# Gathering the transposes of a linear-attention pair behind the next projection, in a fused attention and FFN kernel

## The chip, the cores and the metric

One core of one Trainium2 chip. The metric is the device time of one execution in microseconds; the kernel before ran three times.

## The reference

Attention with a feature map of exponentials, over batch 8, 8 heads, 576 positions and 64 dimensions a head, followed by an FFN on the 4608 tokens (512 to 2048 to 512, with a learned leak `alpha`). All in float32.

```python
def phi(x):
    proj = np.einsum('bhsd,df->bhsf', x, w_phi)
    proj = proj - np.max(np.abs(proj), axis=-1, keepdims=True)
    return np.concatenate([np.exp(proj), np.exp(-proj)], axis=-1)
q_p, k_p = (phi(q), phi(k))
kv = np.einsum('bhsf,bhsd->bhfd', k_p, v)
z = np.sum(k_p, axis=2)
num = np.einsum('bhsf,bhfd->bhsd', q_p, kv)
den = np.einsum('bhsf,bhf->bhs', q_p, z)[..., None] + 1e-06
attn = num / den
...
h = x @ w_in
g = np.maximum(h, 0.0) + alpha * np.minimum(h, 0.0)
out = g @ w_out
```

## The kernel before, in words

**Attention** goes pair by pair: 32 pairs of two heads (`i` from 0 to 31). A pair's k and q come in one tile of nine times 128 columns, and `project(0)` and `project(1)` multiply them with `w_phi`. `project(0)` makes the first eight k tiles (two heads of four, into `pj`), `project(1)` the rest of k and all of q. VectorE takes the row maxima of the absolute values and subtracts them; ScalarE takes the exponentials of k (`k_exp`). `k_z` and `k_acc` then sum z and accumulate kv in one PSUM bank, `kv_out` copies that bank to `ks` on ScalarE, `kv_turn` transposes its three 128x128 blocks on TensorE (L380), and `kv_copy` copies the result to `sf`. `q_turn(0..2)` transposes the ten q blocks (L391, L394), four, four and two, and `q_exp` takes their exponentials straight out of PSUM into `qf`. A visit later `den` and `num` multiply `sf` with `qf`; `den` goes by way of DRAM to be inverted and spread, and GpSimd multiplies it in.

**The FFN** has its 16 hidden blocks in two parts. Five of them are computed during the attention phase, 512 tokens at a time, as `up` and `down` steps of three matmuls each with 512 columns (each value split in a high and a low part; L503 to L505 and L509 to L511). After an `up` ScalarE makes `r` and `g` (two relus, `parts`), VectorE joins them, ScalarE casts to `gh`, VectorE subtracts to `gl`. The other eleven hidden blocks follow when the attention is done, from about 520 us on. Weights are decoded from 64-bit words in between, on ScalarE, VectorE and GpSimd (`decode_*`).

**Order.** Every step is a closure with a time of its own, counted in visits: pair i's steps stand at `i +` the entries of `places(i)` (L57 to L84), the FFN's and the decoder's steps at times of their own. All are sorted by that key (L741, a stable sort of a list in which the pairs stand in order), and TensorE, ScalarE, VectorE and SyncE are pinned to that order. A visit at time t thus does for TensorE: `project(1)` of pair t, `k_z` of t−1, `den` of t−2, `k_acc` of t−1, `num` of t−2, `project(0)` of t+1, and then FFN steps among which the transposes of pair t−1 are strewn:

```python
p=(-0.9955 if early else -0.993, 0.0),
...
kr=1.10,
kc=1.16,
q=(1.34, 1.50, 1.20),
qe=(1.46, 1.62, 1.28),
```

`kr` is `kv_turn`, `kc` `kv_copy`, `q` and `qe` are `q_turn` and `q_exp` for 0, 1 and 2. `early` is i < 9 (`ZP`); the FFN begins at 9.23, so the visits before hold attention alone.

**PSUM** has eight banks of 512 float32 columns: two for the FFN (`psf`), two for `pj`, one for kv (`ps_kv`), and three in a ring (`ps_m`, tag `m`) for the last tiles of `project(1)`, `den`, `num`, and for the late pairs all transposes.

Of the kernel before, what the change touches and what calls it, by code (L numbers as in the profile page):

```python
# [8 lines left out]
F32 = mybir.dt.float32  # L9
# [7 lines left out]
P = 128  # L17
B, H, S, D = 8, 8, 576, 64
FD = 128
# [35 lines left out]
ZP = 9  # L55


def places(i):
    early = i < ZP
    end = i >= NPAIR - 2  # L60
    return dict(
        ld=-1.90,
        lv=-0.80,
        p=(-0.9955 if early else -0.993, 0.0),
        ke=(-0.26, 0.0011),
        ks=(0.0015, 0.0022, 0.0026),
        kz=1.0002,
        ka=1.0012,
        ko=1.0025,
        kr=1.10,  # L70
        kc=1.16,
        q=(1.34, 1.50, 1.20),
        qe=(1.46, 1.62, 1.28),
        d=2.0004,
        ds=2.0008,
        n=2.005,
        s=2.0055,
        d9=2.25,
        dv=3.0016 if early else 3.20 if end else 2.80,
        rd=3.0017 if early else 3.21 if end else 2.82,  # L80
        rr=3.20 if early else 3.45 if end else 3.001,
        x=3.45 if early else 3.60 if end else 3.20,
        xs=3.90 if early else 3.85 if end else 3.45,
    )  # L84
# [24 lines left out]
def fused_kernel(ctx: ExitStack, tc: tile.TileContext, kq, v, w_phi, w_in, w_out, alpha, out):  # L109
    nc = tc.nc  # L110
    act, dve, pool, pe = nc.scalar, nc.vector, nc.gpsimd, nc.tensor
# [18 lines left out]
    psf = ctx.enter_context(tc.tile_pool(name="psf", bufs=2, space=PSUM))  # L130

    ident = cst.tile([P, P], F32, name="ident")
# [122 lines left out]
    ps_m = ps_m_.enter_context(tc.tile_pool(name="ps_m", bufs=3, space=PSUM))  # L255
# [4 lines left out]
    st = att.enter_context(tc.tile_pool(name="st", bufs=2))  # L260
    ps_pj = att.enter_context(tc.tile_pool(name="ps_pj", bufs=1, space=PSUM))
    ps_kv = att.enter_context(tc.tile_pool(name="ps_kv", bufs=1, space=PSUM))
# [9 lines left out]
    def attention_units(i):  # L272
        b, hp = divmod(i, NP)
        c = {}
# [79 lines left out]
                    )  # L354

        def k_z():
            c["kv"] = ps_kv.tile([P, 3, FD], F32, tag="kv", name=f"kv{i}")
            if i < ZP:
                zs = [c["x", 0][:, :, :, j, :] for j in range(4)] + [c["x", 1][:, :, :, 0, :]]
            else:  # L360
                zs = [c["z"]]
            for j, z in enumerate(zs):
                for g in range(4):
                    h, a = divmod(g, 2)
                    pe.matmul(  # L365
                        c["kv"][32 * g : 32 * g + 32, 2],
                        lhsT=ones,
                        rhs=z[:, a, h, :],
                        start=j == 0,
                        stop=j == len(zs) - 1,  # L370
                    )

        def kv_out():
            c["ks"] = st.tile([P, 3, FD], F32, tag="ks", name=f"ks{i}", bufs=1)
            act.copy(c["ks"], c["kv"])

        def kv_turn():
            ps = c["kt"] = ps_m.tile([P, 3, P], F32, tag="m", name=f"kt{i}")
            for j in range(3):
                pe.transpose(ps[:, j, :], c["ks"][:, j, :], ident)  # L380

        def kv_copy():
            c["st"] = st.tile([P, 3, P], F32, tag="sf", name=f"sf{i}")
            act.copy(c["st"], c["kt"])

        def q_turn(h):
            pp, tag = (psf, "f") if i < ZP - 1 and h < 2 else (ps_m, "m")
            ps = c["qt", h] = pp.tile([P, 2 if h == 2 else 4, P], F32, tag=tag, name=f"qt{i}_{h}")
            if h == 2:
                for g in range(2):  # L390
                    pe.transpose(ps[:, g, :], c["t", 1][:, g, 0, :], ident)  # L391
            else:
                for j in range(4):
                    pe.transpose(ps[:, j, :], c["t", 1][:, h, 1 + j, :], ident)  # L394

# [69 lines left out]
        def store():  # L465
            nc.sync.dma_start(x_d[hp, :, b * S : (b + 1) * S], c["s"])

        at = places(i)
        us = [
            (at["ld"], load),  # L470
            (at["lv"], load_v),
            (at["ka"], k_acc),
            (at["kz"], k_z),
            (at["ko"], kv_out),
            (at["kr"], kv_turn),
            (at["kc"], kv_copy),
            (at["n"], num),
            (at["d"], den),
# [11 lines left out]
        for n in range(3):  # L490
            us.append((at["ks"][n], lambda n=n: k_sum(n)))
            us.append((at["q"][n], lambda n=n: q_turn(n)))
            us.append((at["qe"][n], lambda n=n: q_exp(n)))
# [308 lines left out]
```

## Time and profile before

| what | us |
|---|---|
| median of 3 runs | 1137.34 |
| lowest and highest | 1134.79, 1138.68 |
| the profiled execution | 1136.66 |
| its span, first to last instruction | 1134.9 |

The profile is of one execution. The spans of matmuls overlap, since they are pipelined and their ends are modelled; how TensorE's time is spent is read from start to start. PE is TensorE's matmuls, PEld its weight loads, DVE VectorE, ACT ScalarE, POOL GpSimd, SP SyncE, which only issues transfers. In the rows `h`, `o` are the FFN's tiles, `kt` and `qt` the transposed kv and q, `n` is `num`, `pj` the k tiles. L127 and L123 are helpers that every subtraction of a high part and every cast has in common.

### The profile page before, as it was taken

How to read it: one execution, taken by the hardware profiler on the slowest of the kernel's cores; microseconds unless marked ns; L12 is line 12 of the kernel's file. 1: busy time of each engine (PE TensorE's matmuls, PEld its weight loads, DVE VectorE, ACT ScalarE, POOL GpSimd, SP SyncE). 2: the span in 40 equal slices, each digit the busy share in tenths (PEclk: the TensorE clock that was granted, in tenths of full speed). 3: DMA queues.
4: the chain of work that ended last, by engine and by line, in shares of the span. 5: the costliest groups of instructions: out<-in, count | busy, mean ns of one | idle time of the engine just before them, and what ended most of it. 6: DMA issues, size and time to landing. Idle time of an engine off the chain costs nothing.

```text
span 1134.9 us, 18362 instructions
## 1 busy us (share of the span) xinstructions
PE 1114.9 (98%) x7232; PEld 866.8 (76%) x7232; DVE 639.5 (56%) x978; ACT 561.2 (49%) x1149; POOL 214.5 (19%) x219
## 2 busy tenths in 40 slices
PE   7999999999999999999999999999999999999998
PEld 5766777777777777677778888888888888888886
DVE  7888867798788877835762432424242433333323
ACT  4777656666666765664553332424333333333332
POOL 1345332322424142243552000000000000000000
PEclk8999999999999999999999999999999999999999
DMA  5466264556446365466626130303030302020021
GB/s 188 142 184 216 80 194 147 171 163 205 145 163 199 94 214 168 146 197 213 231 74 211 69 112 1 111 1 111 1 112 1 111 1 80 33 79 33 3 72 38
DMA packets 74101, 133.68 MB, mean 118 GB/s; under 512 B 14624, under 2 KB 24480, under 8 KB 73376
## 3 DMA queue, kind: packets, MB, share of 16 engines
q1 hardware_dynamic: 71712, 122.48, 33.4%
q0 software_dynamic: 2016, 9.96, 2.6%
q8 instruction: 57, 0.93, 0.3%
q14 instruction: 28, 0.23, 0.1%
q10 hardware_dynamic: 288, 0.07, 0.0%
HBM read 93.92 MB, written 38.42 MB: 117 GB/s over the span
## 4 chain that ended last, share of the span: by engine, by line
PE 92%; DVE 4%; DMA 2%; ACT 1%; issue 0%; SPq 0%; ACTq 0%; DVEq 0%
PE h L503 11%; PE h L505 11%; PE h L504 11%; PE po L511 8%; PE po L509 8%; PE po L510 8%; PE kv L348 6%; PE pj L307 5%; PE n L413 5%; PE o L511 3%; PE o L509 3%; PE o L510 3%; PE d L431 3%; PE qt L394 2%; PE kv L365 2%; PE pl L307 1%
## 5 line engine op out<-in xcount | busy, mean ns | idle before, releaser
L240 DVE SCALAR_TENSOR_TENSOR g<-r,aln,g 128x512 f32<-128x512 f32 x144 | 111.0, 771 | 320.1 <-ACT g L236 319.8
L235 ACT ACTIVATE r<-h 128x512 f32<-128x512 f32 x144 | 86.5, 601 | 286.0 <-PE h L505 285.8
L127 DVE TENSOR_TENSOR gl<-g,gh 128x512 fp32r<-128x512 f32 x144 | 105.5, 732 | 73.0 <-ACT gh L123 72.5
L123 ACT CAST gh<-g 128x512 fp32r<-128x512 f32 x144 | 90.1, 625 | 88.1 <-DVE g L240 88.1
L236 ACT ACTIVATE g<-h 128x512 f32<-128x512 f32 x144 | 85.8, 596 | 2.8 <-DMA part_d<-os 2.8
L509 PE MATMUL po<-gh,wd 128*128 128x512 f32 x216 | 84.3, 390 | 0.0
L511 PE MATMUL po<-gl,wd 128*128 128x512 f32 x216 | 84.3, 390 | 0.0
L510 PE MATMUL po<-gh,wd 128*128 128x512 f32 x216 | 84.3, 390 | 0.0
L311 DVE TENSOR_REDUCE m<-pj 128x8 f32<-128x1024 f32 (+1 forms) x66 | 78.2, 1185 | 7.0 <-PE pj L307 6.7
L307 PE MATMUL pj<-w_sb,raw 64*128 64x128 f32 x1024 | 74.2, 286 | 7.8 <-DMA w_sb<-w_phi_dram 4.1
L307 PEld LDWEIGHTS pj<-w_sb,raw 64*128 64x128 f32 x1024 | 65.0, 194 | 21.4 <-issue 14.1
L189 POOL TENSOR_TENSOR aw<-ew,aw 128x256 f32<-128x256 f32 x64 | 56.7, 887 | 128.6 <-DVE ew L184 128.6
L312 DVE TENSOR_TENSOR t<-pj,m 128x1024 f32<-128x1024 f32 (+1 forms) x66 | 78.7, 1192 | 2.3
L509 PE MATMUL o<-gh,w 128*128 128x512 f32 x180 | 75.9, 422 | 1.9 <-ACT os L554 1.7
L503 PE MATMUL h<-xh,w 128*128 128x512 f32 x180 | 75.8, 421 | 0.0
L463 POOL TENSOR_TENSOR s<-s,rr 128x576 f32<-128x576 f32 x32 | 48.5, 1517 | 140.6 <-DMA rr<-rec_d 120.2
L511 PE MATMUL o<-gl,w 128*128 128x512 f32 x180 | 71.6, 398 | 3.2 <-DVE gl L127 3.0
L511 PE MATMUL po<-gl,w 128*128 128x512 f32 x180 | 70.3, 391 | 1.5 <-DVE gl L127 1.4
L404 ACT ACTIVATE qf<-qt 128x512 f32<-128x512 f32 x128 | 68.5, 616 | 6.3 <-PE qt L394 6.3
L505 PE MATMUL h<-xl,w 128*128 128x512 f32 x180 | 70.7, 393 | 0.0
L510 PE MATMUL o<-gh,w 128*128 128x512 f32 x180 | 70.6, 392 | 0.0
L504 PE MATMUL h<-xh,w 128*128 128x512 f32 x180 | 70.5, 392 | 0.0
(105 smaller groups left out, 2408.8 us busy)
## 6 DMA issues: line engine op xcount, KB each, us to landing
xr<-x_d SPq DMA_DIRECT2D x18, 1024.0 KB
raw<-kq_dram SPq DMA_DIRECT2D x31, 576.0 KB
v<-v_dram SPq DMA_DIRECT2D x32, 320.0 KB
w_d<-raww SPq DMA_DIRECT2D x38, 256.0 KB
rr<-rec_d SPq DMA_DIRECT2D x64, 144.0 KB
x_d<-s SPq DMA_DIRECT2D x32, 288.0 KB
part_d<-os SPq DMA_DIRECT2D x36, 256.0 KB
pt<-part_d SPq DMA_DIRECT2D x9, 1024.0 KB
```

The costliest lines, as they stand in the source:

```text
L123: return act.copy(dst, src)
L127: return eng.tensor_tensor(dst, src, f(hi), op=ALU.subtract)
L235: act.activation(st["r"], ps, AF.Relu, scale=-1.0)
L236: act.activation(st["g"], ps, AF.Relu)
L240: dve.scalar_tensor_tensor(g, st["r"], aln[:, ff : ff + 1], g, op0=ALU.mult, op1=ALU.add)
L307: pe.matmul(dst[h, j], lhsT=c["raw"][hs, ts], rhs=w_sb[hs], start=True, stop=True)
L503: pe.matmul(ps, lhsT=wt[0][:, ws], rhs=xh, start=n == 0, stop=False)
L504: pe.matmul(ps, lhsT=wt[1][:, ws], rhs=xh, start=False, stop=False)
L505: pe.matmul(ps, lhsT=wt[0][:, ws], rhs=xl, start=False, stop=n == NK - 1)
L509: pe.matmul(ps, lhsT=wt[2][:, ws], rhs=gh, start=first, stop=False)
L510: pe.matmul(ps, lhsT=wt[3][:, ws], rhs=gh, start=False, stop=False)
L511: pe.matmul(ps, lhsT=wt[2][:, ws], rhs=gl, start=False, stop=last)
```

## The change

For pairs from 9 on, `kv_turn`, `q_turn` and `kv_copy` get keys between 1.0070 and 1.0074, and the exponentials of q the keys 1.10, 1.20 and 1.32. The two transposed blocks of kv and the two of q's third group share one four-slot tile `kq` in the ring; the transposed z goes to a fourth slot that the tile in kv's bank gets, and `kv_copy` becomes two copies. For pairs before 9 keys and steps stay as they were, with `kt` and the third `qt` now being parts of four-slot tiles.

```diff
-        kr=1.10,
-        kc=1.16,
-        q=(1.34, 1.50, 1.20),
-        qe=(1.46, 1.62, 1.28),
+        kr=1.10 if early else 1.0070,
+        kc=1.16 if early else 1.0074,
+        q=(1.34, 1.50, 1.20) if early else (1.0072, 1.0073, 1.0071),
+        qe=(1.46, 1.62, 1.28) if early else (1.20, 1.32, 1.10),
...
         def k_z():
-            c["kv"] = ps_kv.tile([P, 3, FD], F32, tag="kv", name=f"kv{i}")
+            c["kv"] = ps_kv.tile([P, 4, FD], F32, tag="kv", name=f"kv{i}")
...
         def kv_out():
             c["ks"] = st.tile([P, 3, FD], F32, tag="ks", name=f"ks{i}", bufs=1)
-            act.copy(c["ks"], c["kv"])
+            act.copy(c["ks"], c["kv"][:, 0:3])
 
         def kv_turn():
-            ps = c["kt"] = ps_m.tile([P, 3, P], F32, tag="m", name=f"kt{i}")
+            c["kq"] = ps_m.tile([P, 4, P], F32, tag="m", name=f"kq{i}")
             for j in range(3):
-                pe.transpose(ps[:, j, :], c["ks"][:, j, :], ident)
+                pe.transpose(c["kv"][:, 3] if j == 2 and i >= ZP else c["kq"][:, j], c["ks"][:, j, :], ident)
 
         def kv_copy():
             c["st"] = st.tile([P, 3, P], F32, tag="sf", name=f"sf{i}")
-            act.copy(c["st"], c["kt"])
+            if i < ZP:
+                act.copy(c["st"], c["kq"][:, 0:3])
+                return
+            act.copy(c["st"][:, 0:2], c["kq"][:, 0:2])
+            act.copy(c["st"][:, 2], c["kv"][:, 3])
 
         def q_turn(h):
-            pp, tag = (psf, "f") if i < ZP - 1 and h < 2 else (ps_m, "m")
-            ps = c["qt", h] = pp.tile([P, 2 if h == 2 else 4, P], F32, tag=tag, name=f"qt{i}_{h}")
             if h == 2:
+                if i < ZP:
+                    c["kq"] = ps_m.tile([P, 4, P], F32, tag="m", name=f"qt{i}_{h}")
+                ps = c["qt", h] = c["kq"][:, 2:4]
                 for g in range(2):
                     pe.transpose(ps[:, g, :], c["t", 1][:, g, 0, :], ident)
             else:
+                pp, tag = (psf, "f") if i < ZP - 1 else (ps_m, "m")
+                ps = c["qt", h] = pp.tile([P, 4, P], F32, tag=tag, name=f"qt{i}_{h}")
```

## Rows read from the trace of the kernel before

**Rows 1.** The page's busy times: engine, us, share of the span, instructions.
```profile
PE 1114.9 (98%) x7232; PEld 866.8 (76%) x7232; DVE 639.5 (56%) x978; ACT 561.2 (49%) x1149; POOL 214.5 (19%) x219
```

**Rows 2.** TensorE's waits, 120 to 520 us: total us, times, longest.
```profile
PE o L511 <- DVE gl L127: 2.5, 3, 1.5
```

**Rows 3.** TensorE's timeline, a late visit: start, us, line, tiles, count.
```profile
313.08 2.11 PE L413 MATMUL n<-qf,sf 128*64 128x288 f32 x16
315.12 1.16 PE L307 MATMUL pj<-w_sb,raw 64*128 64x128 f32 x16
316.21 0.50 PE L503 MATMUL h<-xh,w 128*128 128x512 f32 x1
316.55 0.39 PE L504 MATMUL h<-xh,w 128*128 128x512 f32 x1
316.78 0.39 PE L505 MATMUL h<-xl,w 128*128 128x512 f32 x1
317.01 0.49 PE L380 MATMUL kt<-ident,ks 128*128 128x128 f32 x3
317.25 0.48 PE L503 MATMUL h<-xh,w 128*128 128x512 f32 x1
317.57 0.39 PE L504 MATMUL h<-xh,w 128*128 128x512 f32 x1
```

**Rows 4.** TensorE's timeline, an early visit without FFN steps.
```profile
61.95 2.16 PE L413 MATMUL n<-qf,sf 128*64 128x288 f32 x16
64.04 0.55 PE L380 MATMUL kt<-ident,ks 128*128 128x128 f32 x3
64.42 0.38 PE L391 MATMUL qt<-ident,t 128*128 128x128 f32 x2
64.64 1.04 PE L394 MATMUL qt<-ident,t 128*128 128x128 f32 x8
65.61 0.49 PE L307 MATMUL pl<-w_sb,raw 64*128 64x128 f32 x4
```

**Rows 5.** Busy us (count) of PE, PEld, DVE, ACT, POOL; PEclk; DMA; GB/s.
```profile
60.50:65.50 5.00, 5.00 (x49) 3.43 (x45) 3.83 (x5) 2.49 (x8) 1.10 (x2) 1.00 0.67 179
```

**Rows 6.** ScalarE's timeline, the copies out of kv's bank in three late visits.
```profile
123.83 0.46 ACT L375 COPY ks<-kv 128x384 f32<-128x384 f32 x1
...
296.78 0.48 ACT L375 COPY ks<-kv 128x384 f32<-128x384 f32 x1 [0.26 <-PE kv L348]
...
448.73 0.46 ACT L375 COPY ks<-kv 128x384 f32<-128x384 f32 x1
```

**Rows 7.** TensorE's timeline, the k tiles of the same three visits.
```profile
124.14 1.16 PE L307 MATMUL pj<-w_sb,raw 64*128 64x128 f32 x16
...
298.60 1.16 PE L307 MATMUL pj<-w_sb,raw 64*128 64x128 f32 x16
...
448.12 1.16 PE L307 MATMUL pj<-w_sb,raw 64*128 64x128 f32 x16 [0.15 <-DVE t L312]
```

**Rows 8.** ScalarE's and TensorE's timelines, a wait for the copy in pair 7.
```profile
97.38 0.46 ACT L375 COPY ks<-kv 128x384 f32<-128x384 f32 x1
...
97.89 0.55 PE L380 MATMUL kt<-ident,ks 128*128 128x128 f32 x3 [0.83 <-ACT ks L375]
```

**Rows 9.** TensorE's timeline, three waits; in brackets the idle time and its releaser.
```profile
152.10 0.50 PE L509 MATMUL o<-gh,w 128*128 128x512 f32 x1 [1.72 <-ACT os L554]
...
402.51 0.50 PE L511 MATMUL o<-gl,w 128*128 128x512 f32 x1 [0.17 <-DVE gl L127]
...
470.65 0.50 PE L511 MATMUL o<-gl,w 128*128 128x512 f32 x1 [1.54 <-DVE gl L127]
```

**Rows 10.** ScalarE's and VectorE's timelines, ahead of two late copies of kv.
```profile
187.78 1.12 ACT L404 ACTIVATE qf<-qt 128x512 f32<-128x512 f32 x2
...
192.63 0.75 DVE L240 SCALAR_TENSOR_TENSOR g<-r,aln,g 128x512 f32<-128x512 f32 x1 [1.50 <-ACT g L236]
...
443.27 0.69 DVE L127 TENSOR_TENSOR gl<-g,gh 128x512 fp32r<-128x512 f32 x1 [3.65 <-ACT gh L123]
```

## The prediction

> **What bounds the kernel now.** I read the page's busy times first: TensorE is busy for 98% of the span, ScalarE for 49% [rows 1]. So a nanosecond between two matmuls is a nanosecond of the result, and work on the other engines counts only where TensorE waits for it. Next I read TensorE's waits from 120 to 520 us, the stretch in which the change acts: the longest entry is 2.5 us in three waits [rows 2], and one more of 1.72 us stands on the timeline [rows 9]. There is little idle time to win. What remains is the spacing of matmuls, so the rest is read on the timeline of starts, not from busy times, whose ends are modelled.
>
> **Where the moved steps land.** The order of all four pinned queues is that of the sorted keys. For pair i, `kv_turn` gets i + 1.0070. `project(0)` of pair i+2, the next k tiles, has i + 2 − 0.993, which is the same number in floating point for all 21 pairs from 9 to 29 (I worked the additions out). The sort is stable and pair i's units were appended first, so the three kv transposes come *ahead of* the k tiles, right behind `num`, and the ten q transposes behind them. FFN matmuls follow without a break. For pairs 30 and 31 no k tiles follow. Twenty-three visits change.
>
> **Seams.** In a late visit now [rows 3]: `num` to the k tiles 2.04 us (313.08 to 315.12), k tiles to the first FFN matmul 1.09, first to second FFN matmul 0.34 against an ordinary 0.23. The three kv transposes stretch the two FFN steps around them from 0.46 to 0.79 (316.78 to 317.57): 0.33. The three q groups, read the same way, cost 0.23, 0.44 and 0.44. Sum 2.04 + 1.09 + 0.34 + 1.44 = 4.91 us.
>
> The new order exists in the trace already: in the early visits no FFN runs, and 13 transposes stand in one run before the k tiles [rows 4]. `num` to transposes is 2.09 us there; I take 2.04, since the late `num` does not follow k tiles and loses the 0.05 that a first step behind them shows. Transposes are 0.11 apart (two in 0.22), the first three take 0.38 (0.33 and 0.05 of seam), and eight take 0.97 to the k tiles (0.88 and 0.09). So: 2.04; three transposes 0.38 + 0.09 = 0.47; k tiles 1.09; ten transposes 1.10 + 0.05, less the 0.09 by which an FFN matmul follows a last transpose sooner (three take 0.24 to it [rows 3]), 1.06; first to second FFN matmul 0.32 (317.25 to 317.57). Sum 4.98: **+0.07 us** in each of 21 visits. A transpose costs 0.11 wherever it stands, so gathering them removes almost nothing. The two last visits, by the same terms with one run of 13 and no k tiles: 3.75 against 3.82, −0.07 each. Seams: 21 × 0.07 − 0.14 = +1.3 us. Bounds: 0.01 of reading on each of seven terms, so 0 to 0.14 a visit, 0 to +3.
>
> **The wait of the kv transposes.** They read `ks`, the ScalarE copy out of kv's bank, and TensorE now reaches them where the k tiles began, 1.9 us earlier (315.12 for 317.01 [rows 3]). An early visit shows this very wait: copy over at 97.38 + 0.46 = 97.84, transposes at 97.89 [rows 8]; 0.05 of latency, 0.83 idle. Everything on TensorE stands behind it: k tiles, q transposes, FFN. In 18 of the 23 visits the copy would be over in time, typically at 297.26 where TensorE is free at 298.60 [rows 6, 7]. In five it is late: from the first (123.83 + 0.46 + 0.05 = 124.34 against 124.14, 0.20) to the last (449.24 against 448.12, 1.12), sum 3.07 us over the five [rows 6, 7]; the three between are 0.52, 0.90 and 0.28.
>
> Does the lateness stay? `ks` stands on ScalarE behind the next pair's `k_exp(1)`, which waits for VectorE's subtraction, which stands behind the FFN's join. Where VectorE waits for ScalarE because `q_exp(1)` lay in the second half of the visit, it goes: at 187.78 that exp runs for 1.12 us ahead of the FFN's relus, and the join at 192.63 has waited 1.50 for ScalarE [rows 10]. `q_exp(1)` now runs earlier, about 1 us comes free there, and 0.90 of lateness goes; the same holds for the 0.52 and the 0.28. In the last one VectorE waited 3.65 us for the cast of `gh` [rows 10], which stands behind `k_exp(0)` and a relu that waited for TensorE itself; nothing moves, and 1.1 us stays. The first comes before any moved exp and stays, 0.20. I take +1.1 (the 0.20 is absorbed below); bounds 0 and 3.1.
>
> **What the old waits give back.** The wait at 152.10 (1.72 us) is for an output copy that stands on ScalarE behind a cast of a tile being fetched [rows 9]; its end is set by a transfer, so up to that point the seams of two visits and the 0.20 vanish in it: −0.14 of seams. At 402.51 (0.17 idle) and 470.65 (1.54 idle) TensorE waits for `gl` from VectorE in the middle of a visit [rows 9], with the two four-transpose groups still to come. These 0.88 us now come before, and fill the waits: −0.2 and −0.9. VectorE gets the k tiles 0.47 later, but TensorE comes to `gl` later by more. Sum −1.1, bounds 0 and −1.7.
>
> **Costs taken as nothing.** z's own copy adds one ScalarE instruction a visit, at most the 0.46 of the wider `ks` copy; ScalarE is 49% busy and its next user of `sf` is a visit away. The four-slot tiles still fit a 512-column bank. The ring of three banks has eight takers for nine; q's first group takes the bank of `num`'s first half, freed by copies that stand right behind `ks`, two of them at under 0.46, while TensorE comes there 0.47 + 1.09 + 0.27 us after the kv transposes. The three exps now stand ahead of more FFN relus in ScalarE's queue, but so do their transposes on TensorE. No moved step issues a transfer; SP's and POOL's queues keep their order. If ScalarE's cover failed, the FFN's casts would be late next, and TensorE would wait in `gl` again.
>
> **Sum.** 1.3 − 0.14 + 1.1 − 1.1 = +1.2 us on the profiled execution's 1136.66 us (span 1134.9 and 1.8 around it): 1137.9. The median of the runs, 1137.34, lies 0.7 above that execution: **1138.5 us**. Anything under 0.3%, 3.4 us, is no change for this kernel.
>
> **Rivals.** *The kv wait grows (slower).* TensorE waits in order for `ks` at the end of `num`. Seams 1.3, all five waits 3.1, nothing given back: 4.4 us, 1141.7. For it: the waits are there in this trace. Against: `q_exp(1)` comes off the critical half. It decides from 2.1 us of wait on top of the seams. Chance 0.11. *The order is the other one*: all 13 transposes behind the k tiles. Then the 0.47 and a second seam go: (2.04 + 1.09 + 0.05 + 1.43 − 0.09 + 0.32) − 4.91 = −0.07 a visit, no wait: −1.6 − 1.1, 1134.6; still within 0.3%. The stable sort speaks against it: 0.05. *All waits go (faster).* ScalarE, relieved early, ends TensorE's 2.5 and 1.7 us and nothing new appears; with seams at their lower bound of 0: −4.2, 1133.1. The 1.7 hangs on a transfer: 0.04. *The run of transposes costs the clock*: ten in a row, and TensorE falls from 2.4 to 1.2 GHz; their 1.1 us double in 23 visits, +25, 1163. The trace speaks against it: the window with 13 in a row has a granted clock of 1.00 [rows 5]: 0.02. The Trainium skill (TensorE: Matmul & The Clock Gate, Part 4: PE-mode transpose) says that the full clock doesn't engage for transposes, which would favour this last rival. By that rule it would be 1163, by the row no change; these short runs between matmuls don't show it.
>
> **Numbers.** My forecast holds 0.78, within 0.3%; its own range is 1136 to 1140.5. Faster 0.04, same 0.78 + 0.05 = 0.83, slower 0.11 + 0.02 = 0.13. The range takes in the other order and the persisting waits: 1134.5 to 1141.2.
>
> **What would show it.** After: kv transposes between `num` and k tiles, ten q transposes 0.11 apart behind them; 16.5 us from visit to visit as before; no `gl` wait near 402, under 0.8 near 470; one wait of the kv transposes for `ks` near 449, none above 0.3 near 142, 198 and 315. It is wrong if kv transposes wait in most visits, if FFN matmuls behind the run keep to 0.3 us, or if the granted clock falls.

## The result, and the profile after

The changed kernel takes 1139.26 us (median of 20 runs), the kernel before 1137.28 beside it: 1.0018 of before, 95% interval [1.0011, 1.0025]. That is +2.0 us where +1.2 was forecast, inside the 0.3% and inside the range. One run of 1399.57 us among the twenty, at a mean granted clock of 0.755, is out of the ratio.

The profiled execution took 1141.63 us, with a span of 1139.9 against 1134.9; it is the slowest of the nineteen runs that remain. 0.8 us of its 5.0 had gone before the first moved step: the first k matmul of pair 9's visit starts at 100.29 against 99.46, on code that did not change. What follows is read behind that point.

A late visit after, on TensorE's timeline (start, us, line, tiles, count):

```profile
300.30 2.11 PE L420 MATMUL n<-qf,sf 128*64 128x288 f32 x16
302.34 0.44 PE L380 MATMUL kq<-ident,ks 128*128 128x128 f32 x2
302.61 0.27 PE L380 MATMUL kv<-ident,ks 128*128 128x128 f32 x1
302.81 1.16 PE L307 MATMUL pj<-w_sb,raw 64*128 64x128 f32 x16
303.91 0.44 PE L396 MATMUL kq<-ident,t 128*128 128x128 f32 x2
304.18 1.04 PE L401 MATMUL qt<-ident,t 128*128 128x128 f32 x8
304.97 0.48 PE L510 MATMUL h<-xh,w 128*128 128x512 f32 x1
305.29 0.39 PE L511 MATMUL h<-xh,w 128*128 128x512 f32 x1
...
311.99 0.49 PE L307 MATMUL pl<-w_sb,raw 64*128 64x128 f32 x4
...
328.54 0.49 PE L307 MATMUL pl<-w_sb,raw 64*128 64x128 f32 x4
```

The kv transposes stand ahead of the k tiles, as the equal keys said, and the q transposes behind them. The terms are those of the forecast: 2.04; 0.47 for three transposes up to the k tiles; 1.10; 1.06 for ten up to the FFN; 0.32. From one visit to the next it is 16.55 us (311.99 to 328.54). Before it was 16.52, on the same timeline of the kernel before:

```profile
308.23 0.49 PE L307 MATMUL pl<-w_sb,raw 64*128 64x128 f32 x4
...
324.75 0.49 PE L307 MATMUL pl<-w_sb,raw 64*128 64x128 f32 x4
```

So the seams cost +0.03 us a visit. TensorE's waits from 112 to 532 us of the kernel after (total, times, longest), to set beside [rows 2]; the window ends later, since the last steps of the attention phase stand about 5 us later than before:

```profile
PE o L516 <- ACT os L561: 3.3, 2, 1.7
PE kq L380 <- ACT ks L375: 3.1, 3, 1.3
PE o L518 <- DVE gl L127: 2.0, 3, 1.4
```

The line of `ks` is new, and so is one of the two waits for `os`, at 530.03. All of them on the timeline:

```profile
144.05 0.44 PE L380 MATMUL kq<-ident,ks 128*128 128x128 f32 x2 [0.78 <-ACT ks L375]
...
154.07 0.50 PE L516 MATMUL o<-gh,w 128*128 128x512 f32 x1 [1.64 <-ACT os L561]
...
200.17 0.44 PE L380 MATMUL kq<-ident,ks 128*128 128x128 f32 x2 [1.04 <-ACT ks L375]
...
341.14 0.50 PE L518 MATMUL o<-gl,w 128*128 128x512 f32 x1 [0.29 <-DVE gl L127]
...
453.18 0.44 PE L380 MATMUL kq<-ident,ks 128*128 128x128 f32 x2 [1.27 <-ACT ks L375]
...
476.55 0.50 PE L518 MATMUL o<-gl,w 128*128 128x512 f32 x1 [1.40 <-DVE gl L127]
...
523.73 0.50 PE L518 MATMUL o<-gl,w 128*128 128x512 f32 x1 [0.30 <-DVE gl L127]
...
530.03 0.50 PE L516 MATMUL o<-gh,w 128*128 128x512 f32 x1 [1.67 <-ACT os L561]
```

From start to start the kv transposes are late by 0.18, 0.85, 1.10 and 1.34 us in four visits, 3.5 in sum. The brackets give a little less, since the modelled ends of matmuls cover the beginning of a wait. The waits of [rows 9] are hardly smaller: 1.64 for 1.72 and 1.40 for 1.54; the small one near 402 is gone, and one of 0.29 has come near 341. The third wait for `gl` in [rows 2], which [rows 9] do not show, went from 0.78 to 0.30; before it stood here:

```profile
519.58 0.50 PE L511 MATMUL o<-gl,w 128*128 128x512 f32 x1 [0.78 <-DVE gl L127]
```

The granted clock did not fall in the changed visits of this execution: a window over the moved transposes has 1.00 (busy us and count of PE, PEld, DVE, ACT, POOL; clock; DMA share; GB/s).

```profile
302.00:307.00 5.00, 5.00 (x42) 4.03 (x39) 3.14 (x5) 3.02 (x9) 1.41 (x1) 1.00 0.97 363
```

The wait at 530.03 goes back to GpSimd. TensorE, ScalarE, VectorE and SyncE are pinned to the sorted keys, GpSimd is not, and its order changed. Before, the decoding of weights (`aw`) stood ahead of the multiplication `s`, which waits for a transfer:

```profile
517.27 1.11 POOL L189 TENSOR_TENSOR aw<-ew,aw 128x256 f32<-128x256 f32 x1 [1.22 <-DVE ew L184]
521.85 1.43 POOL L463 TENSOR_TENSOR s<-s,rr 128x576 f32<-128x576 f32 x1 [3.47 <-DMA rr<-rec_d]
```

After, it stands behind it, and on ScalarE the cast that needs `aw` stands ahead of the copies to `os`:

```profile
526.94 1.43 POOL L470 TENSOR_TENSOR s<-s,rr 128x576 f32<-128x576 f32 x1 [6.20 <-DMA rr<-rec_d]
528.33 0.72 POOL L189 TENSOR_TENSOR aw<-ew,aw 128x256 f32<-128x256 f32 x1
529.08 0.40 ACT L123 CAST raww<-aw 128x256 fp32r<-128x256 f32 x1 [5.36 <-POOL aw L189]
529.39 1.07 ACT L561 COPY os<-o 128x512 f32<-128x512 f32 x2
```

This new order is in the traces of all kernels below in which q's steps moved, and in none of the others. No run changed it alone.

### The profile page after: what moved, and what is told of

It reads as the page before. It is cut to its first block, busy times and chain, and to the rows that moved or that the text cites. A ratio compares the mean times of both kernels' runs of the same rounds, so it can differ in the third digit from the quotient of the medians.

```text
span 1139.9 us, 18357 instructions
## 1 busy us (share of the span) xinstructions
PE 1115.8 (98%) x7232; PEld 870.0 (76%) x7232; DVE 640.5 (56%) x978; ACT 563.1 (49%) x1172; POOL 215.9 (19%) x219
## 4 chain that ended last, share of the span: by engine, by line
PE 85%; DVE 6%; DMA 4%; ACT 3%; issue 1%; POOL 0%; SPq 0%; DVEq 0%; ACTq 0%; POOLq 0%
PE h L510 10%; PE h L512 10%; PE h L511 10%; PE po L518 8%; PE po L516 8%; PE po L517 8%; PE kv L348 5%; PE pj L307 5%; PE n L420 4%; PE o L518 3%; PE o L516 3%; PE o L517 3%; PE d L438 2%; PE qt L401 2%; PE kv L365 1%; DVE m L311 1%
## 5 line engine op out<-in xcount | busy, mean ns | idle before, releaser
L516 PE MATMUL o<-gh,w 128*128 128x512 f32 x180 | 72.1, 401 | 3.4 <-ACT os L561 3.3
L510 PE MATMUL h<-xh,w 128*128 128x512 f32 x180 | 71.7, 398 | 0.0
L517 PE MATMUL o<-gh,w 128*128 128x512 f32 x180 | 70.2, 390 | 0.0
L516 PE MATMUL po<-gh,w 128*128 128x512 f32 x180 | 70.1, 389 | 0.0
L511 PE MATMUL h<-xh,w 128*128 128x512 f32 x180 | 70.1, 389 | 0.0
```

Source lines behind the costliest of these rows:

```text
L510: pe.matmul(ps, lhsT=wt[0][:, ws], rhs=xh, start=n == 0, stop=False)
L511: pe.matmul(ps, lhsT=wt[1][:, ws], rhs=xh, start=False, stop=False)
L516: pe.matmul(ps, lhsT=wt[2][:, ws], rhs=gh, start=first, stop=False)
L517: pe.matmul(ps, lhsT=wt[3][:, ws], rhs=gh, start=False, stop=False)
```

## The experiments

Each ratio is to the kernel before, run on the same chip in turns. "Lateness" below is how long after the end of `num` plus an ordinary step the copy `ks` can be used, worked out from ScalarE's and TensorE's timelines for the 23 visits and added up where it is positive.

**All transposes behind the k tiles.** One key of the changed kernel:

```diff
-        kr=1.10 if early else 1.0070,
+        kr=1.10 if early else 1.00705,
```

> The changed kernel, with the three kv transposes put strictly behind the k tiles (key 1.00705), so that all 13 stand in one run. Theory (the loss is TensorE's in-order wait for ks ahead of the k tiles, about 3 us over four visits): the wait goes, the seam goes from +0.03 to about -0.09 us a visit, and the kernel takes 1.0 to 3.0 us less than the changed one needs more than before, so 0.997 to 1.000 of before. Rival (the loss is the later FFN work on ScalarE and VectorE, or the seams, whatever the place of the kv transposes): 1.001 to 1.003 as the changed kernel.

0.9995 [0.9984, 1.0007]; in a second set of runs 0.998 [0.9969, 0.9992]:

> The kernel with all 13 transposes behind the k tiles and the shared tile once more, beside kv's own bank on the same chip: 0.999 to 1.000 if the own bank is worth 1.5 us; 0.998 to 0.999, as the other, if the first difference was spread.

The wait for `ks` is gone from its list (112 to 530 us):

```profile
PE o L516 <- ACT os L561: 4.4, 2, 2.8
PE o L518 <- DVE gl L127: 2.2, 3, 1.6
PE pj L307 <- DVE t L312: 0.2, 1, 0.2
```

The copies are as late as in the changed kernel (3.5 us in sum), but the k tiles now cover it. A visit is 0.12 us shorter than before (0.07 was worked out for this order), 16.40 us:

```profile
308.19 0.49 PE L307 MATMUL pl<-w_sb,raw 64*128 64x128 f32 x4
...
324.59 0.49 PE L307 MATMUL pl<-w_sb,raw 64*128 64x128 f32 x4
```

Against that the wait for `os` near 153 is 2.8 us instead of 1.7, and the one of GpSimd's order is there too, with 1.6 near 523.

**Only the kv transposes moved.** The kernel before, with two keys:

```diff
-        kr=1.10,
-        kc=1.16,
+        kr=1.10 if early else 1.0070,
+        kc=1.16 if early else 1.0074,
```

> The kernel before, with only the kv transposes and their copy moved (keys 1.0070 and 1.0074), q as before. Theory of the wait: 3 us of wait and a seam of under 0.1 us a visit, so +2 to +5 us, 1.002 to 1.004. Rival (q's move is what costs): 1.000, within 0.001.

1.0034 [1.0022, 1.0047], more than the whole change, though the intervals overlap. Lateness is 3.2 us, all of it now waited for, and a visit is 0.15 us longer (294.37 to 311.04), where under 0.1 was expected.

```profile
PE kt L380 <- ACT ks L375: 2.7, 4, 1.3
...
294.37 0.49 PE L307 MATMUL pl<-w_sb,raw 64*128 64x128 f32 x4
...
311.04 0.49 PE L307 MATMUL pl<-w_sb,raw 64*128 64x128 f32 x4
```

**Only the q transposes moved.**

```diff
-        q=(1.34, 1.50, 1.20),
-        qe=(1.46, 1.62, 1.28),
+        q=(1.34, 1.50, 1.20) if early else (1.0072, 1.0073, 1.0071),
+        qe=(1.46, 1.62, 1.28) if early else (1.20, 1.32, 1.08),
```

> The kernel before, with only the q transposes and exponentials moved (keys 1.0072, 1.0073, 1.0071 and 1.20, 1.32, 1.08; the last one 0.02 earlier than in the change so that the ring of banks stays in order), kv as before among the FFN steps. Theory of the wait: no wait of the kv transposes, so 0.999 to 1.001. Rival (exponentials ahead of the FFN's relus delay ScalarE and then VectorE): +2 us or more, 1.002 and over.

1.0011 [0.9999, 1.0023]: between the two, and the interval does not separate them. A visit is 0.11 us shorter, but a wait for `gl` near 473 grew to 2.6 us. Around its end the granted clock is 0.50 (1.2 GHz) from 472.4 to 475.8 us. The twelve runs have a mean granted clock of 0.9959, the runs of the kernel before beside them 0.9975, so a part of the time here may be the clock's. The copies to `ks` are late by 4.8 us in sum, but the kv transposes stand late enough not to wait.

**The copy to `ks` ahead of the exponential.** The changed kernel; the next pair's second `k_exp` behind `kv_out`:

```diff
-        ke=(-0.26, 0.0011),
+        ke=(-0.26, 0.0011 if i <= ZP else 0.00255),
```

> The changed kernel, with the copy to ks ahead of the next pair's second k exponentials on ScalarE (their key 0.00255 instead of 0.0011 from pair 10 on). Theory (ks is late because it queues on ScalarE behind an exponential that waits for VectorE): the kv transposes wait nowhere after pair 9, and some 3 us go: 0.999 to 1.000 of before. Rival (ks is late for another reason, or the wait is made up elsewhere): the wait or the time stays, 1.001 to 1.003.

1.0001 [0.9988, 1.0014]; the interval just touches that of the changed kernel. On ScalarE's timeline the copy now waits for kv alone, and the exponential waits for VectorE's `t` behind it; the same visit as that of the wait at 200.17 above:

```profile
195.24 0.48 ACT L375 COPY ks<-kv 128x384 f32<-128x384 f32 x1 [1.88 <-PE kv L348]
197.02 0.73 ACT L320 ACTIVATE k<-t 64x256 f32<-64x256 f32 x2 [1.30 <-DVE t L312]
```

Lateness is 0 in all 23 visits and the line of `ks` is gone from the waits, with the kv transposes where the change put them. A visit stays at +0.03, and the waits for `os` stay (2.7 near 152, 1.3 near 525). Of these runs this is the cleanest on the wait for `ks`, since neither the seams nor the places on TensorE differ from the changed kernel's.

**The exponentials where they were.** The changed kernel with the old keys `qe=(1.46, 1.62, 1.28)` for all pairs.

> The changed kernel with q's exponentials at the keys that they had (1.46, 1.62, 1.28). The forecast said that exponentials moved ahead free ScalarE late in the visit and so take lateness off ks; the first runs speak against it. Theory now (ScalarE is as late at the end of a visit either way): the copies to ks that are late stay late by 3 to 4.5 us in sum, and the time is 1.001 to 1.003 of before. Rival (the earlier exponentials did take lateness off): lateness over 5 us, 1.003 to 1.005.

1.0029 [1.0018, 1.0039], and the lateness is 6.4 us in six visits. By the lateness the rival was right, and the theory stated there fell: the earlier exponentials do take lateness off, as far as one execution of each kernel shows. The time lies between the two ranges.

```profile
PE kq L380 <- ACT ks L375: 5.9, 5, 1.8
```

This execution also shows what a wait can bring with it. Behind the longest of these waits (1.78 us, until 452.75) the granted clock fell to 0.50, which is 1.2 GHz, from 454.25 on. The same window in it (first line) and in the changed kernel (second):

```profile
454.30:457.60 3.30, 3.30 (x15) 3.07 (x14) 3.08 (x5) 1.19 (x4) 0.73 (x1) 0.50 0.00 0
...
454.30:457.60 3.30, 3.30 (x28) 2.87 (x25) 3.10 (x5) 1.63 (x7) 0.74 (x1) 1.00 0.00 0
```

TensorE started about half as many matmuls. From `num` to the next `num` this takes 19.95 us, 18.09 without the 1.86 that the kv transposes were late, against 17.89 and 16.55 in the changed kernel: an estimate of 1.5 us for the clock, nearly as much as the wait. The same happened with the wait of 2.6 us above and once behind a wait for `os` (2.5 us, then 0.50 from 152.7 to 156.1 in the second run with kv's own bank). It did not behind the 2.8 us of the first experiment or the 1.3 us of the changed kernel; no rule for it is shown here.

**The fetch early.** The second FFN tile's input fetched 0.14 of a visit sooner:

```diff
-        todo += ffn1_units(b, FG if t1 < TL else GL)(t0, t1, t0 - (FL if b else FL0), [t0 - dt for dt in (FX if b else FX0)])
+        todo += ffn1_units(b, FG if t1 < TL else GL)(t0, t1, t0 - (FL0 if b == 0 else 1.54 if b == 1 else FL), [t0 - dt for dt in (FX if b else FX0)])
```

On the changed kernel:

> The changed kernel with the fetch of the second FFN tile's input 0.14 of a visit earlier (1.54 instead of 1.40 before that tile's start), so that on SP's queue it stands ahead of pair 8's reciprocal, not behind it. Theory (the wait of 1.6 to 2.8 us for the output copy near 153 us hangs on that queue place, so it moved with the visits and absorbed nothing): the wait is gone, and 1 to 2 us go: 0.9995 to 1.0010 of before. Rival (the transfer is bound by bandwidth or by the tile's producer): the wait stays over 1 us, 1.001 to 1.003.

1.0012 [1.0002, 1.0023]: 0.0006 under the changed kernel's own ratio, which the intervals do not tell from nothing, where 1 to 2 us were expected. A miss on the time, although the wait went. On the kernel before:

> The kernel before with nothing but the earlier fetch. Theory (its wait of 1.7 us near 152 hangs on the place in SP's queue): the wait goes under 0.5 us, 0.998 to 0.999 of before. Rival (another wait takes its place): 0.9995 to 1.0005.

0.9969 [0.9958, 0.998], a larger gain than the 0.998 to 0.999 expected. SyncE's queue in the changed kernel, the issue of `xr` held behind the store of a reciprocal (`rec_d`):

```profile
133.67 0.33 SPq L473 DMA_DIRECT2D x_d<-s  x1
144.16 0.33 SPq L460 DMA_DIRECT2D rec_d<-r  x1
144.55 0.43 SPq L279 DMA_DIRECT2D raw<-kq_dram  x1
145.07 0.38 SPq L526 DMA_DIRECT2D xr<-x_d  x1
```

and with the early fetch, in the changed kernel:

```profile
133.51 0.33 SPq L473 DMA_DIRECT2D x_d<-s  x1
135.61 0.38 SPq L526 DMA_DIRECT2D xr<-x_d  x1
144.05 0.32 SPq L460 DMA_DIRECT2D rec_d<-r  x1
```

The wait for `os` near 153 is gone in both (0.4 from start to start for an ordinary 0.23). In the changed kernel the one of GpSimd's order stays, with 1.4 near 528.

**The kv transposes in kv's own bank.** On top of the first experiment: the three turned blocks go back over the copied ones, one copy takes them out, and q's third group has a tile of its own.

```diff
-                pe.transpose(c["kv"][:, 3] if j == 2 and i >= ZP else c["kq"][:, j], c["ks"][:, j, :], ident)
+                pe.transpose((c["kv"] if i >= ZP else c["kq"])[:, j], c["ks"][:, j, :], ident)
...
-            act.copy(c["st"][:, 0:2], c["kq"][:, 0:2])
-            act.copy(c["st"][:, 2], c["kv"][:, 3])
+            act.copy(c["st"], c["kv"][:, 0:3])
```

> All 13 transposes behind the k tiles as in the first run, and the three kv transposes go back into the three slots of kv's own bank, copied out by one instruction; q's third group has a tile of its own. Theory (the copy of the turned kv was held behind q's third group, which shares its tile, but ScalarE's place there costs TensorE nothing): the copy starts 0.2 us and more sooner after the kv transposes, and the time is that of the first run, 0.998 to 1.001. Rival (the hold makes ScalarE late and so the waits for gl): 0.996 to 0.998.

0.9978 [0.9967, 0.999]; in the second set, beside the shared tile (0.998):

> The kernel with kv's own bank once more, beside the shared tile on the same chip: if the own bank is worth 1.5 us, 0.997 to 0.999 and under the other by 0.001 or more; if the first difference was spread, within 0.001 of the other.

0.9986 [0.9972, 1.0]. The first difference was spread; the own bank is worth nothing that these two can tell.

**Both edits.** All transposes behind the k tiles, and the early fetch:

> All 13 transposes behind the k tiles, and the fetch ahead of the reciprocal on SP's queue. If both theories hold, the wait for ks and the wait of 2.8 us near 153 are gone: 0.996 to 0.998 of before. If the fetch only uncovers another wait: 0.999 to 1.000.

0.9954 [0.9942, 0.9967], 1133.05 us, faster than the 0.996 to 0.998 expected. With kv's own bank as well:

> All transposes behind the k tiles, the kv transposes back into kv's own bank, and the fetch early. If releasing the copy of the turned kv from q's third group is worth something by itself, 0.993 to 0.995; if not, as the kernel with both edits but the shared tile, 0.995 to 0.997.

0.9942 [0.9928, 0.9957], 1131.95 us against 1138.11: the fastest version here. By the expectation this lies where the own bank would be worth something, but the interval takes in the 0.9954 of the shared tile; with the direct comparison above, the worth of the own bank stays open. Its waits from 112 to 530 us:

```profile
PE o L517 <- DVE gl L127: 2.4, 4, 1.6
PE o L515 <- ACT os L560: 0.4, 1, 0.4
```

## Why the prediction was right, and where its terms were off

*The order and the seams: right.* The sort put the kv transposes ahead of the k tiles. Every term of the new sequence came out within 0.01 us; +0.07 a visit was worked out and +0.03 measured, 0.04 off, the size that reading seven differences to 0.01 allows. The two last visits got shorter by 0.14 and 0.16 instead of 0.07 each. That gathering transposes buys little is shown by the visit lengths: +0.03 here, +0.15 with kv alone, −0.11 with q alone, −0.12 with all of them behind the k tiles. Over 21 visits the last is 2.5 us, 0.2% of the time, and as large as the effect of the whole change.

*The wait of the kv transposes: right in its mechanism, mis-sized.* This is the largest part of what made the kernel slower. Put behind the k tiles, or with `ks` copied sooner, the wait is gone from the trace and the ratio falls to 0.9995 and 1.0001. I kept 1.1 (and an absorbed 0.2) of 3.1 us; 3.5 came. (The five terms of that sum add up to 3.02, not 3.07. The last of them was read too small: the k tiles from whose start it counts had themselves waited for VectorE [rows 7]. From the end of `num` it is 1.34, before and after.) The failed step is "about 1 us comes free there": 0.90 and 0.52 of lateness were to go, and they came as 1.10 and 0.85. In pair 13's visit ScalarE did not come free. Its timeline after, in the half visit for which [rows 10] gave 187.78:

```profile
186.14 0.60 ACT L235 ACTIVATE r<-h 128x512 f32<-128x512 f32 x1 [0.86 <-PE h L512]
186.63 0.59 ACT L236 ACTIVATE g<-h 128x512 f32<-128x512 f32 x1
187.11 2.07 ACT L411 ACTIVATE qf<-qt 128x512 f32<-128x512 f32 x4
189.02 0.66 ACT L123 CAST gh<-g 128x512 fp32r<-128x512 f32 x1
```

The FFN begins later in the visit, because ten more transposes stand ahead of it; the relus wait for it (0.86), and the exponentials, moved ahead of the cast, push the cast and all that follows back by what they freed. VectorE's two joins in this half visit waited 0.76 and 1.50 us for ScalarE before and 1.37 and 0.52 after, 0.4 less in sum. With the exponentials left late lateness is 6.4, with them early 3.5, before it was 3.2: by these single executions, moving q's transposes made ScalarE late, and moving its exponentials made up for about that. Only the 0.28 near 315 went, as forecast.

*What the old waits give back: wrong.* 1.1 us and an absorbed 0.14 were forecast. The wait for `os` absorbed nothing, because its end moved with the visits. I took the end as set by a transfer, and did not look at what stood ahead of its issue: on SyncE's queue the store of a reciprocal, which waits for VectorE. The fetch put ahead of it removes the wait in both kernels. The wait for `gl` near 470 went from 1.54 to 1.40, not by 0.9: TensorE did come there later, but so did VectorE: its reduction of those k tiles, which it reached without a gap, starts 5.90 us later than before (473.43 for 467.53), while the visit starts 5.08 later. The forecast counted only the 0.47 of the k tiles against it; why VectorE was behind already was not tried. One wait near 402 went and one near 341 came. The 0.5 us that the wait near 520 gave back was in no term.

*A cost taken as nothing: GpSimd's order, wrong.* "SP's and POOL's queues keep their order" holds for SyncE, whose 402 transfers stand as before, and not for GpSimd. Its new order near 527 brought the wait of 1.67 us for `os` at 530.03, which the kernel before does not have. In other executions with this order it was nothing, 0.4, or 1.3 to 3.0 us. In this execution it is about made up by the two last visits (0.3), the wait near 520 (0.5) and two short waits of the kernel before near 544 that went (0.7).

*The sum: near by luck.* Over the 21 visits with k tiles the profiled execution lost 4.1 us (later by 0.83 than before at 100.29, and by 4.97 at 481.08). That is what the forecast's own terms give with measured sizes: 0.6 of seams, 3.5 of waits and about nothing back. The wait was sized too small and the give-back too large; both errors make the forecast too small, and GpSimd's wait does too, so they do not cancel. That the median shows only +2.0, 0.8 from the forecast, the terms do not explain. The two profiled executions lie apart from their medians, 2.4 us above after and 0.6 below before, which is the rest of their 5.0. Single waits differ between executions of one kernel: in the two profiles of the first experiment's kernel those for `os` were 2.8 and 1.6 us, then 2.3 and 3.0, and in the two of the kernel with kv's own bank the second was absent, then 2.8. What part of the 4.1 is this execution alone stays open.

*The signs.* The order, the 16.5 us from visit to visit, the wait near 449 and the missing one near 402 were as forecast. The waits for `ks` near 142 and 198 (0.85 and 1.10 us for "none above 0.3") and the one for `gl` near 470 (1.40 for "under 0.8") were not.

*The rivals.* The slower one, that the kv wait persists whole, is the case that came by its condition: 3.5 us where it decides from 2.1, in four visits instead of five, and about nothing given back. Its time, +4.4, is about what the profiled execution lost there; the median's +2.0 is nearer to the forecast's. The other order was tried: worked out at −2.7 us, measured at −0.6 and −2.3 us in two runs. The clock did not fall for a run of transposes: in the profiles of the changed kernel and of the first experiment, which has runs of thirteen, it is 1.00 over all changed visits. The Trainium skill (TensorE: Matmul & The Clock Gate, Part 4: PE-mode transpose) has the full clock not engage for transposes; these short runs between matmuls do not show it. Where the clock fell in other traces, a wait of 1.8 to 2.6 us stood before it; in one of the three the fall set in 1.5 us behind the wait's end, with 0.50 from about the start of a run of transposes on.

## What to carry to other kernels

Moving work along an in-order engine is priced by what it then waits for: with TensorE 98% busy the spacing was worth 0.03 us a visit, and one operand that was late in four visits of 23 cost 3.5 us in the profiled execution. Work whose own consumer is far off, here a visit away, can stand behind something that waits for nothing, here the k tiles, and its operand's lateness is covered. And before a wait is taken as fixed or as a cushion, look at the queue that issued its transfer: the 1.7 us near 152 were a matter of one place in SyncE's order. By the ratios, changing that place gave 3.5 us on the kernel before, nothing certain on the changed kernel, and 3 to 5 us once all transposes stood behind the k tiles. Last, an engine whose order is not pinned can change its order when others move: compare it in both traces before its cost is put at nothing, and read waits to the end of the stretch that moved.

## What had not been expected

The early fetch alone gave 0.9969 of before, 3.5 us, where its wait is 1.7 us long; the rest is not explained by its own profile, in which other waits for `gl` add up to 3.2 us. Part of it goes with the clock: its eleven runs have a mean granted clock of 0.9991, the 29 of the kernel before beside them 0.9976, and among those 29 the time rises by 0.7 us for every 0.001 that the clock is lower, which by estimate makes 1.1 us of the 3.5. Whether the wait that went had cost clock, as waits did in three of the traces above, or whether these runs drew a better clock, is not shown. And the copy of the turned kv, reading slots that were written before the k tiles, waited for q's third group, which only writes other slots of the same tile: 1.51 to 1.53 us of idle ScalarE in one visit after another, on its timeline after:

```profile
183.88 0.37 ACT L387 COPY sf<-kq 128x256 f32<-128x256 f32 x1 [1.53 <-PE kq L396]
```

With kv's own bank the copy no longer stands behind that group (1.16 us of idle time, for the kv transposes alone); whether the time shows it stays open, as said above.
